# The head of a sorted-attention and gated-MLP kernel: another queue for one load, another order of the first keys, another spread of the first transposes

## The chip, the cores and the metric

The kernel runs on one core of a Trainium2 chip. The metric is the device time of one execution in microseconds. A core has TensorE (PE; its weight loads are listed as PEld), VectorE (DVE), ScalarE (ACT), GpSimd (POOL) and SyncE (SP), each with its own instruction stream in program order. Transfers are issued by SP, ACT and GpSimd and are carried out by 16 DMA engines.

## The reference

Four batches with eight heads each attend within eight blocks of 96 positions. An 8 by 8 matrix per head (`sort_net`) is balanced in five rounds and mixes the blocks of k and v; then every block of q attends to the mixed block of its own number. The result, as 3072 rows of 512, goes through an MLP with the gate h * cos(h).

```python
for _ in range(5):
    P = exp(P - max(P, -1)); P /= sum(P, -1) + 1e-9; P /= sum(P, -2) + 1e-9
k_sorted = einsum('bhij,bhjcd->bhicd', P, k_blocks)      # v the same
attn = softmax(q_blk @ k_sorted.T / sqrt(64))            # per block of 96
x = (attn @ v_sorted)  as [3072, 512]
h = x @ w_in                                             # [3072, 2048]
out = (h * cos(h)) @ w_out                               # [3072, 512]
```

## The kernel before

The 3072 rows are handled in eight groups `n` of 384 rows (one batch, four of its eight blocks). For every group the kernel makes the mixed keys and values it needs, transposes the query, computes scores (`qk`), the softmax (`expo`), the product with the values (`av`), a transpose of the result (`x_transpose`), and the two matrix products of the MLP (`up` and `down`). The order of instructions on every engine is written out by hand: the calls stand in the order in which the engines get their work. PSUM tiles come from two rotating pools, `big` (three tiles of two banks) and `acc` (two tiles of one bank); a new tile waits until the tile that had the buffer has been read.

The head, up to the first scores, is one chain:

- The sort matrices of batches 0 and 1 are loaded as two transfers of 64 rows, one issued on ACT and one on SP (L83), those of batches 2 and 3 as one of 128 rows, behind the first on ACT (L85). All go to `P_a`. VectorE then takes the maximum of each half `g` (L239, first g = 0, then g = 1), and only after that makes the masks from the identity.
- GpSimd issues the load of the first query rows (`load_q(0)`, L123), makes the identity (`make_identity`, in masks.py), issues the loads of k and v of batch 0 (`load`, L92), and clears the tail of three buffers (L195). All loads of GpSimd go through one queue, q0 in the profile.
- The balancing (L330 to L353) runs four passes, `it` = 0 to 3, for both halves: exponentials on ACT, column sums by a product on PE (`product`, L261), reciprocal and scaling on VectorE (`balance`). PE fills the gaps with transposes of the first query (`q_products`, L299; 32 in all, 16 for each half `z` of the heads), which ACT copies to `q_turned` during the last pass. The last pass ends with the spread weights of the first half (`spread(0)`, L280).
- The key blocks of group 0 are mixed on PE (`k_sort_0(t0, nt, engine, pool, tag)`, L361; `t0` and `nt` choose which of the 48 column tiles), and copied from PSUM to `kTs` with four copies per call by the engine named (the copies of ACT have line 286, those of VectorE line 288, whoever calls them). `v_turn` brings the weights for v into place (`bdv`, L437), `v_sort_b` mixes v (L451). `v_permute` on GpSimd (L176) rearranges half of v meanwhile. Then `qk(0, 0)` computes the first scores (L423).

Of the kernel before, what the change touches and what calls it, by code (L numbers as in the profile page):

```python
# [18 lines left out]
def kernel(  # L19
# [15 lines left out]
    nc = tc.nc  # L35
    B, H, S, D = q.shape
# [26 lines left out]
    big = ctx.enter_context(tc.tile_pool(name="big", bufs=3, space=bass.MemoryType.PSUM))  # L63
# [7 lines left out]
    vbuf, kbuf = kv[:, :CD], kv[:, CD:]  # L71
# [10 lines left out]
    for r, b in ((64, 0), (0, 1)):  # L82
        (nc.scalar, nc.sync)[b].dma_start(  # L83
            out=P_a[r:r + 64, 0], in_=sort_net[b].rearrange("h i j -> (h i) j"))
    nc.scalar.dma_start(  # L85
        out=P_a[:, 1], in_=sort_net[2:].rearrange("b h i j -> (b h i) j"))

    kin_d = k.rearrange("b h (j c) d -> b (h j) (c d)", j=nb)
    vin_d = v.rearrange("b h (j c) d -> b (h j) (c d)", j=nb)

    def load(buf, r, src):
        nc.gpsimd.dma_start(out=buf[r:r + 64], in_=src)  # L92
# [16 lines left out]
    def q_zeroed(n):  # L109

        return kbuf[:blk, :2 * (QZ + D)] if n % 2 else q_mem[:]
# [7 lines left out]
    def load_q(n):  # L119
        b, ih = n // 2, n % 2  # L120
        if n < NQ:

            nc.gpsimd.dma_start(  # L123
                out=q_rows, in_=q[b][:, ih * IC * blk:(ih + 1) * IC * blk].rearrange(
                    "h (p r) d -> p h (r d)", r=QR))
        else:
            src = q[b].rearrange("h (i c) d -> c i h d", c=blk).rearrange(
                "c i (h e) d -> c i h e d", e=2)
            q_heads = q_zeroed(n).rearrange("p (e x) -> p e x", e=2)[:, :, :QZ].rearrange(
                "p e (i h w) -> p i h e w", i=IC, h=H2)[:, :, :, :, :D]  # L130
            for i in range(IC):
                for e in range(2):
                    nc.gpsimd.dma_start(  # L133
                        out=q_heads[:, i, :, e], in_=src[:, ih * IC + i, :, e])

    def q_of(n, e):
        return q_turned[n % 2][:, e]
# [17 lines left out]
    def load_w_in(z):  # L155
        c = slice(z * Dff // 4, (z + 1) * Dff // 4)
        nc.gpsimd.dma_start(out=w_in_t[:, :, c], in_=w_in_d[:, :, c])

    def load_w_out(z):
        c = slice(z * FC // 4, (z + 1) * FC // 4)  # L160
        nc.gpsimd.dma_start(out=w_out_t[:, c], in_=w_out_d[:, c])
# [22 lines left out]
    kTs = const.tile([128, 3, 3, NB, HT], BF16, name="kTs")  # L184
    kT, kT2 = [kTs[:, :, 0], kTs[:, :, 2]], kTs[:, :, :2]

    load_q(0)
    make_identity(nc, ident[:])
    load(kbuf, 64, kin_d[0])
    load(vbuf, 0, vin_d[0])  # L190
    NP = 3
    p_bufs = []
    for i in range(NP):
        t = const.tile([blk, 2 * H2, 128], BF16, name=f"p_buf{i}")
        nc.gpsimd.memset(t[:, :, blk:], 0.0)  # L195
        p_bufs.append(t)
    vS[0] = const.tile([blk, 4 * NB, VW], BF16, name="vS")
    vS[1] = pair[:blk].rearrange("p (x w) -> p x w", w=VW)

# [59 lines left out]
    def product(lhs, rhs):  # L259
        ps = acc.tile([128, nb], FP32, name="sk", tag="acc")  # L260
        nc.tensor.matmul(  # L261
            ps[:], lhs.rearrange("p x j -> p (x j)"), rhs, start=True, stop=True)
        return ps
# [15 lines left out]
    def spread(g):  # L279
        nc.vector.scalar_tensor_tensor(  # L280
            bds[g][:], maskp.to_broadcast([128, 2 * H, nb]), ci[g][:], along(T[g]),
            op0=ALU.mult, op1=ALU.mult)

    def copy_on(eng, dst, src):
        if eng is nc.scalar:
            eng.copy(dst, src)  # L286
        else:
            eng.tensor_copy(dst, src)  # L288

    V, A = nc.vector, nc.scalar  # L290
# [3 lines left out]
    def q_products(n, z, lo, hi, pool, tag):  # L294
        if lo == 0:
            q_ps[n, z] = pool.tile([128, 2, IC, QR, blk // QR], BF16, name="qps", tag=tag)
        for i in range(lo, hi):
            e, hp, r = i // (2 * QR), i // QR % 2, i % QR
            nc.tensor.transpose(  # L299
                q_ps[n, z][hp * D:(hp + 1) * D, e, :, r],  # L300
                q_rows[:, (z * 2 + e) * 2 + hp, r * D:(r + 1) * D], ident[:blk, :blk])

    def q_turn(n, z, pool, tag, lo=0):
        q_products(n, z, lo, 4 * QR, pool, tag)
        ps = q_ps.pop((n, z))

        def place(hp, rows):
            dst = q_of(n, hp)[rows, :QW].rearrange("d (i h c) -> d h i c", h=H2, c=blk)
            return dst[:, z * 2:z * 2 + 2], ps[rows].rearrange("d e i r p -> d e i (r p)")

        if n == 0:
            return [place(0, slice(0, 128))]
        return [place(hp, slice(hp * D, (hp + 1) * D)) for hp in range(2)]
# [5 lines left out]
    def balance(g):  # L319

        nc.vector.scalar_tensor_tensor(
            T_eps[g][:], E_eps[g][:], 1.0, rr_one[g][:], op0=ALU.mult, op1=ALU.mult,
            accum_out=cs[g][:])
        nc.vector.reciprocal(ci[g][:], cs[g][:])
# [3 lines left out]
    for it in range(4):  # L328
        for g in range(NG):
            nc.scalar.activation(E[g], T[g], AF.Exp, scale=ci[g][:])  # L330
        nc.vector.tensor_copy(seen[:], E[0][:, :1])
        if it == 3:
            copy_on(A, *turned[0])
        sk = [product(same, E[g]) for g in range(NG)]
        if it == 1:
            q_products(0, 0, 0, 10, big, "big")
        elif it == 2:
            turned = q_turn(0, 0, big, "big", 10)
            q_products(0, 1, 0, 4, big, "big")
        elif it == 3:  # L340
            turned = q_turn(0, 1, big, "big", 4)
            copy_on(A, *turned[0])
        if it == 1:

            nc.gpsimd.tensor_copy(held[:], cs[1][:])
            for z in range(3):
                load_w_in(z)
            load_w_out(0)
        for g in range(NG):
            nc.vector.reciprocal(rr[g], sk[g][:])  # L350
            if it < 3 or g == 0:
                balance(g)
                if it == 3:  # L353
                    spread(0)
# [5 lines left out]
    def k_products(ps, t, c, rows, rhs, keys=kbuf):  # L360
        nc.tensor.matmul(  # L361
            ps[:, t], keys[rows, c * 2 * D:(c + 1) * 2 * D], rhs, start=True, stop=True)

    def k_sort_0(t0, nt, eng, pool, tag):

        ps = pool.tile([128, nt, 2 * MH], FP32, name="ks", tag=tag)
        for t in range(nt):
            k_products(ps, t, t0 + t, slice(64, 128),
                       bds[0][64:, H:, :IC])
        ms, ts = slice(0, MH), slice(t0, t0 + nt)  # L370
        psv = ps.rearrange("p t (e m) -> p e m t", e=2)
        for hp in range(2):
            for x in range(2):
                copy_on(eng, kT[0][hp * D:(hp + 1) * D, hp + x, ms, ts],
                        psv[x * D:(x + 1) * D, hp])
# [58 lines left out]
    def v_turn(eng=A):  # L434
        ps = big.tile([128, 128], FP32, name="bdp", tag="big")
        for r in (0, 64):
            nc.tensor.matmul(  # L437
                ps[r:r + 64], ident[:, 64 - r:128 - r], bds[0].rearrange("p x i -> p (x i)"),
                start=True, stop=True)
        copy_on(eng, bdv.rearrange("p x i -> p (x i)"), ps[:])  # L440
# [4 lines left out]
    def v_sort_b(b, d0, nd, eng, pool, tag):  # L445
        ps = pool.tile([128, nd, 2 * NB], FP32, name="vs", tag=tag)


        rows, xs = slice(0, 64 + b * 64), slice((1 - b) * H, (2 - b) * H)
        for t in range(nd):  # L450
            nc.tensor.matmul(  # L451
                ps[:, t], v_cols(d0 + t, b == 1 or d0 + t >= D // 2)[rows],
                bdv[rows, xs].rearrange("p x i -> p (x i)"), start=True, stop=True)
        copy_on(
            eng, vS[0][:, b * 2 * NB:(b + 1) * 2 * NB, d0:d0 + nd],
            ps[:blk].rearrange("p t n -> p n t"))
# [207 lines left out]
    B, C = (big, "big"), (acc, "acc")  # L664
# [27 lines left out]
        next(wz)  # L692

    k_sort_0(40, 8, V, *B)
    k_sort_0(0, 16, V, *C)
    v_turn()
    load_q(1)
    k_sort_0(32, 8, V, *B)
    load_w_in(3)
    k_sort_0(16, 16, A, *B)  # L700
    v_sort_b(0, 0, 8, A, *B)
    load_w_out(1)
    qk(0, 0)
# [241 lines left out]
```

## Time and profile before

| | us |
|---|---|
| median of 3 runs | 239.96 (239.51 to 241.65) |
| profiled execution, its own time | 241.18 |
| its span | 239.40 |
| PE busy in the span | 226.0 (94%) |
| VectorE busy | 175.8 (73%) |
| ACT busy | 155.3 (65%) |
| GpSimd busy | 87.7 (37%) |
| bytes read from and written to HBM | 27.27 and 6.29 MB |

All times of the trace count from the start of the span. A row of the timeline gives start, duration (of all instructions that were merged, if there are several), engine, line, operation, what is written and read, how many, and in brackets the idle time of the engine before it with what ended it. SPq, ACTq and POOLq rows are the issuing of transfers. A row of the chain of waits gives start, length, and the work that the end of the span waited for in that time.

### The profile page before, as it was taken

The page shows a single profiled execution, that of the slowest core. Times are in us where ns is not written, and L with a number is a line of the kernel's source. Part 1 is how long each engine was busy: PE and PEld are TensorE (multiplying, and loading weights), DVE is VectorE, ACT ScalarE, POOL GpSimd, SP SyncE. Part 2 cuts the span into 40 slices and gives each one's busy share as a digit, 9 for nine tenths or more (in the row PEclk, how much of TensorE's full clock was granted, in tenths as well). Part 3 has the DMA queues.
Part 4 walks back from the last instruction along what each step waited for, and adds up shares of the span by engine and source line. Part 5 has one row for each costly group of instructions (what it writes and reads, how often), then busy time and mean ns, then how long its engine had stood idle before and what let it go on. Part 6 is the DMA issues. An engine that isn't in the chain of part 4 may idle for free.

```text
span 239.4 us, 5344 instructions
## 1 busy us (share of the span) xinstructions
PE 226.0 (94%) x2148; PEld 148.1 (62%) x2169; DVE 175.8 (73%) x325; ACT 155.3 (65%) x217; POOL 87.7 (37%) x110
## 2 busy tenths in 40 slices
PE   2797999999999999999999999999999999999994
PEld 0777788956766566656566565655565566456554
DVE  3678977698879976895768986897789769635700
ACT  4355967785688946888578947683667376737611
POOL 6469953896960056990726200800000000000000
PEclk9999999999999999999999999999999999999999
DMA  6999999992999259786889769926671450251012
GB/s 82 213 198 205 207 210 219 212 158 89 132 152 162 66 138 191 122 179 154 117 115 126 79 136 140 189 43 99 136 212 33 102 181 0 49 140 44 0 47 89
DMA packets 66681, 30.90 MB, mean 129 GB/s; under 512 B 55392, under 2 KB 62176, under 8 KB 66400
## 3 DMA queue, kind: packets, MB, share of 16 engines
q0 software_dynamic: 24048, 13.64, 41.1%
q1 hardware_dynamic: 42096, 16.72, 29.8%
q8 instruction: 17, 0.28, 0.5%
q10 hardware_dynamic: 512, 0.20, 0.3%
q14 instruction: 8, 0.07, 0.1%
HBM read 27.27 MB, written 6.29 MB: 140 GB/s over the span
## 4 chain that ended last, share of the span: by engine, by line
PE 85%; DVE 7%; DMA 3%; ACT 2%; issue 1%; ACTq 0%; DVEq 0%
PE h L597 34%; PE o L629 31%; PE sc L428 4%; PE av L546 4%; PE ks L361 2%; DVE kTs L288 2%; PE xps L573 2%; PE pps L533 2%; PE vs L461 2%; DMA P_a<-in_sort_net_dram 2%; PE o L909 1%; PE sk L261 1%; PE qps L299 1%; DMA vperm<-p_buf 1%; PE vs L451 1%
## 5 line engine op out<-in xcount | busy, mean ns | idle before, releaser
L597 PE MATMUL h<-xT,w_in_t 128*128 128x384 bf16 (+1 forms) x576 | 91.2, 310 | 0.4 <-DVE xn L555 0.3
L629 PE MATMUL o<-w_out_t,gg 128*128 128x512 bf16 x347 | 85.1, 379 | 1.1
L604 ACT ACTIVATE c<-h,half_pi 128x768 f32<-128x768 f32 (+1 forms) x68 | 58.6, 864 | 26.8 <-PE h L597 25.6
L612 DVE TENSOR_TENSOR gg<-c,h 128x768 bf16<-128x768 f32 (+1 forms) x64 | 57.1, 899 | 22.2 <-ACT c L604 22.2
L597 PEld LDWEIGHTS <-w_in_t 128*128 128x128 bf16 x576 | 53.1, 98 | 27.1 <-issue 1.0
L629 PEld LDWEIGHTS <-gg 128*128 128x128 bf16 x368 | 33.1, 98 | 30.9
L489 DVE TENSOR_TENSOR s<-sc,mx 96x384 f32<-96x384 f32 (+1 forms) x43 | 32.2, 749 | 2.3
L483 DVE TENSOR_REDUCE mx<-sc 96x4 f32<-96x384 f32 (+1 forms) x43 | 31.9, 741 | 1.4 <-PE sc L428 0.7
L176 POOL COPY vperm<-kv 64x1536 bf16<-64x1536 bf16 (+1 forms) x10 | 28.0, 2843 | 1.1 <-DMA kv<-in_v_dram 1.1
L507 ACT ACTIVATE p_buf<-s 96x768 bf16<-96x768 f32 x32 | 26.0, 840 | 3.2 <-DVE s L489 2.9
L555 DVE TENSOR_TENSOR xn<-av,r 96x512 bf16<-96x512 f32 x32 | 22.0, 686 | 1.1
L133 POOL DMA_DIRECT2D kv<-in_q_dram x24 | 15.9, 671 | 0.8 <-issue 0.8
L428 PE MATMUL sc<-kTs,q_turned 128*128 128x96 bf16 x224 | 15.6, 206 | 0.0
L428 PEld LDWEIGHTS <-q_turned 128*128 128x128 bf16 x224 | 12.8, 98 | 4.0 <-DVE s L489 0.4
L553 DVE RECIPROCAL r<-av 96x8 f32<-96x8 f32 x32 | 6.4, 199 | 11.6 <-PE av L546 11.5
L286 ACT COPY kv<-o 128x512 f32<-128x512 f32 (+2 forms) x10 | 5.3, 531 | 14.3 <-PE o L629 12.7
L286 ACT CAST kTs<-ks 128x512 bf16<-128x512 f32 (+1 forms) x21 | 11.2, 539 | 3.7 <-PE ks L361 3.7
L133 POOL DMA_DIRECT2D q_mem<-in_q_dram x16 | 10.7, 684 | 2.6 <-DMA kv<-in_v_dram 2.3
L288 DVE COPY kv<-o 128x512 f32<-128x512 f32 (+1 forms) x5 | 3.0, 602 | 11.4 <-PE o L909 8.6
L286 ACT COPY xT<-xps 128x384 bf16<-128x384 bf16 (+1 forms) x10 | 5.1, 511 | 9.1 <-PE xps L573 9.1
L604 ACT ACT_TABLE_LOAD x8 | 10.3, 1283 | 0.1
L286 ACT COPY o_s<-o 128x512 f32<-128x512 f32 x9 | 5.3, 586 | 7.4 <-PE o L629 7.2
(105 smaller groups left out, 230.6 us busy)
## 6 DMA issues: line engine op xcount, KB each, us to landing
out_dram<-kv SPq DMA_DIRECT2D x12, 256.0 KB, 2.7
out_dram<-o_s SPq DMA_DIRECT2D x11, 256.0 KB, 2.4
w_in_t<-in_moe_w_in_dram POOLq DMA_DIRECT2D x4, 512.0 KB, 8.7
w_out_t<-in_moe_w_out_dram POOLq DMA_DIRECT2D x4, 512.0 KB, 12.6
kv<-in_k_dram POOLq DMA_DIRECT2D x2, 768.0 KB, 9.0
kv<-in_v_dram POOLq DMA_DIRECT2D x2, 768.0 KB, 12.5
pair<-in_k_dram POOLq DMA_DIRECT2D x2, 768.0 KB, 12.3
kv<-in_v_dram POOLq DMA_DIRECT2D x6, 256.0 KB, 6.3
```

The lines of the kernel that those rows point to most:

```text
L133: nc.gpsimd.dma_start(out=q_heads[:, i, :, e], in_=src[:, ih * IC + i, :, e])
L176: nc.gpsimd.tensor_copy(dst, src)
L286: eng.copy(dst, src)
L428: nc.tensor.matmul(out, q_of(n, hp)[:, x:x + 128], keys_of(n, u, h2, hp), start=True, stop=True)
L483: nc.vector.reduce_max(mx[:], scv, axis=AX.X)
L489: nc.vector.tensor_tensor(s, scv, mx.to_broadcast(list(s.shape)), op=ALU.subtract)
L507: nc.scalar.activation(p[:, :, :blk], s_t.pop((n, u)).rearrange("p e h c -> p (e h) c"), AF.Exp, scale=scale)
L555: nc.vector.tensor_tensor(xn.rearrange("p h e d -> p e h d"), avv[:, :, :, :D], r.to_broadcast([blk, 2, H2, D]), op=ALU.mult)
L597: nc.tensor.matmul(to, w_in_t[:, kk, f * 128:(f + 1) * 128], xT[n][:, kk, lo:hi], start=(kk == 0), stop=(kk == KC - 1))
L604: nc.scalar.activation(c[:, :, :x], h[:, :, :x], AF.Sin, bias=half_pi[:, 0:1])
L612: nc.vector.tensor_tensor(gate(n, fp)[:, :, lo:hi], c[:, :, :x], h[:, :, :x], op=ALU.mult)
L629: nc.tensor.matmul(o[:], gate(n, f // 2)[:, f % 2, ts * 128:(ts + 1) * 128], w_out_t[:, f, :], start=(f == 0), stop=(f == FC - 1))
```

## The change

Three things are changed.

- The third load of the sort matrix (L85) is issued by SP, behind SP's first, and not by ACT.
- `load_q(0)` and the loads of k and v are issued after the identity and after the clearing of the first of the three buffers; the other two are cleared after the loads. The loads keep their order.
- The transposes of the first query are spread as 4, 12, 10 and 6 over the passes 0 to 3, where it was 0, 10, 10 and 12. The order of the first keys is 40, 16, then the weights for v, then 0 and 32 (first column tile of each call), where it was 40, 0, weights, 32, 16. VectorE copies 40 and 0 and the weights for v, ACT copies 16 and 32; before, VectorE copied 40, 0 and 32, ACT the weights and 16. Calls 0 and 32 take their PSUM tiles from `acc`, 40 and 16 from `big`; before, only 0 was in `acc`. On GpSimd the order of instructions behind the first loads stays the same.

```diff
-    nc.scalar.dma_start(
+    nc.sync.dma_start(
         out=P_a[:, 1], in_=sort_net[2:].rearrange("b h i j -> (b h i) j"))
...
-    load_q(0)
     make_identity(nc, ident[:])
-    load(kbuf, 64, kin_d[0])
-    load(vbuf, 0, vin_d[0])
     NP = 3
     p_bufs = []
     for i in range(NP):
         t = const.tile([blk, 2 * H2, 128], BF16, name=f"p_buf{i}")
         nc.gpsimd.memset(t[:, :, blk:], 0.0)
         p_bufs.append(t)
+        if i == 0:
+            load_q(0)
+            load(kbuf, 64, kin_d[0])
+            load(vbuf, 0, vin_d[0])
...
-        if it == 1:
-            q_products(0, 0, 0, 10, big, "big")
+        if it == 0:
+            q_products(0, 0, 0, 4, big, "big")
+        elif it == 1:
+            turned = q_turn(0, 0, big, "big", 4)
         elif it == 2:
-            turned = q_turn(0, 0, big, "big", 10)
-            q_products(0, 1, 0, 4, big, "big")
+            q_products(0, 1, 0, 10, big, "big")
         elif it == 3:
-            turned = q_turn(0, 1, big, "big", 4)
+            turned = q_turn(0, 1, big, "big", 10)
             copy_on(A, *turned[0])
...
     k_sort_0(40, 8, V, *B)
+    k_sort_0(16, 16, A, *B)
+    load_q(1)
+    v_turn(V)
+    load_w_in(3)
     k_sort_0(0, 16, V, *C)
-    v_turn()
-    load_q(1)
-    k_sort_0(32, 8, V, *B)
-    load_w_in(3)
-    k_sort_0(16, 16, A, *B)
+    k_sort_0(32, 8, A, *C)
     v_sort_b(0, 0, 8, A, *B)
```

## The prediction

> **What bounds the kernel now.** I read the span by stages first, then the chain of waits, then the start in order of time.
>
> The view by stretches (time, then busy time of PE, PEld, DVE, ACT, POOL, granted clock, DMA share, GB/s) separates two regimes:
>
> ```profile
> 14.79:19.45 4.66, 2.92 (x60) 2.46 (x60) 4.00 (x12) 3.12 (x7) 4.66 (x3) 1.00 1.25 209
> 48.00:239.40 191.40, 186.82 (x1635) 113.79 (x1654) 141.10 (x215) 125.45 (x162) 54.95 (x64) 1.00 0.63 113
> ```
>
> From 48 us on, matrix work fills 186.82 of 191.40 us: nothing in the diff touches that part, so it can only be shifted. Between 14.79 and 19.45, where the first keys are made, VectorE is busy for 4.00 of 4.66 us and PE for 2.92. The chain of waits (start, length, what) says what holds this stretch and the one before it:
>
> ```profile
> 1.36 3.64 DMA P_a<-in_sort_net_dram
> 5.01 0.02 issue
> 5.03 0.16 DVE nmx L239
> ...
> 14.08 0.78 PE qps L299 x12
> ...
> 15.22 0.28 DVE kTs L288
> ...
> 19.45 0.49 PE sc L423 x7
> ```
>
> The chain begins with the third load of the sort matrix, passes twelve transposes of the query that stand ahead of the first keys, and then twelve VectorE copies of keys in a row. All three are on the path, so a microsecond taken there is one off the start of everything behind, unless something there is held by another clock (a transfer, GpSimd).
>
> **The third load.** It is issued at 1.36 on ACT, behind another; on SP it stands behind a load whose issue ends at 0.74 + 0.58 = 1.32, so it leaves no earlier than now. What changes is its company. DMA issues with microseconds to landing, then the packets, MB and share between 3 and 4 us (q0 carries GpSimd's loads, q10 ACT's):
>
> ```profile
> q_mem<-in_q_dram POOLq DMA_DIRECT2D x1, 384.0 KB, 5.6
> P_a<-in_sort_net_dram SPq DMA_DIRECT2D x1, 2.0 KB, 2.1
> P_a<-in_sort_net_dram ACTq DMA_DIRECT2D x1, 4.0 KB, 3.6
> ```
> ```profile
> q0 software_dynamic: 100, 0.05, 54.6%
> q10 hardware_dynamic: 26, 0.00, 3.5%
> ```
> ```profile
> 0.74 0.58 SPq L83 DMA_DIRECT2D P_a<-in_sort_net_dram  x1
> 0.82 0.06 DVE L206 MEMSET half_pi<- 128x1 f32 x1 [0.82 <-PEq L929]
> 1.30 0.90 POOL L123 DMA_DIRECT2D q_mem<-in_q_dram  x1 [0.85 <-POOLq L929]
> 1.36 0.86 ACTq L85 DMA_DIRECT2D P_a<-in_sort_net_dram  x1
> 2.50 0.29 POOL masks.py:199 TENSOR_SCALAR_AFFINE_SELECT ident<-ident 128x128 bf16<-128x128 bf16 x1
> 3.79 0.84 POOL L195 MEMSET p_buf<- 96x256 bf16 x3
> ```
>
> The small load on SP (L83) landed after 2.1 us, the third after 3.6, with its packets between the query's. In the changed kernel GpSimd first makes the identity (from the end of the query's issue, 1.30 + 0.90 = 2.20, to 2.50 + 0.29 = 2.79: 0.59) and clears one buffer (0.84 / 3 = 0.28), so the query's load leaves 0.87 later at most, at 2.17. GpSimd may start before 1.30, where it ends 0.85 us of idle time, since VectorE is let go at 0.82; then the query's load leaves as early as 0.82 + 0.59 + 0.28 = 1.69, 0.39 later. Either way the third load's packets have most of the engines to themselves. From both sides: with the small load's 2.1 plus the longer issue (0.86 - 0.58 = 0.28) it lands at 1.35 + 2.4 = 3.75; with nothing gained, at 1.35 + 3.64 = 4.99. I take 3.85, near the first end, because the rows to which it is then alike are the undisturbed ones: VectorE's first reduction moves from 5.03 to 3.87, **1.16 us**. ACT loses an issue of 0.86, which was covered by the same wait, so this counts nothing.
>
> [...]
>
> **The query's turns.** Per transpose: 0.78 / 12 = 0.065. Before, 10, 10 and 12 stood in passes two to four; now 4, 12, 10 and 6 in passes one to four.
>
> ```profile
> 9.33 1.18 PE L261 MATMUL sk<-E,same 128*128 128x8 f32 x4 [0.64 <-ACT E L330]
> 10.44 0.69 PE L299 MATMUL qps<-ident,q_mem 96*64 96x96 bf16 x10
> ```
> ```profile
> 14.15 0.35 DVE L280 SCALAR_TENSOR_TENSOR bd<-maskp,ci,T 128x128 bf16<-128x128 f32 x1
> 14.79 0.39 PE L361 MATMUL ks<-bd,kv 64*128 64x32 bf16 x8
> 14.89 0.80 ACT L286 COPY q_turned<-qps 128x768 bf16<-128x768 bf16 x1 [0.78 <-PE qps L299]
> 15.90 0.27 ACT L286 CAST bdv<-bdp 128x128 bf16<-128x128 f32 x1 [0.20 <-PE bdp L437]
> 16.84 1.50 ACT L286 CAST kTs<-ks 64x256 bf16<-64x256 f32 x4 [0.68 <-PE ks L361]
> ```
>
> The spread weights are ready at 14.50, yet the first key product starts at 14.79, behind the twelve. Six end at 14.08 + 0.39 = 14.47: product at 14.54, **0.25 gained**. The second pass gets two more than the ten that began at 10.44, 0.13 ahead of the third pass's products; the fourth pass has ten in front of it in either kernel, so much of this is waited for anyway, and I count 0.05 of the 0.13. The four of the first pass (0.26) fit into PE's idle 0.64 ahead of 9.33, if the query has landed: it lands at 1.69 to 2.17 plus 5.6 = 7.3 to 7.8, wanted at 9.33 - 1.16 - 0.26 = 7.9. That cover is thin; behind it stand the next products and with them both halves of the balancing. I put 0.1 for it.
>
> **The keys.** By shapes (mean ns last before the idle time):
>
> ```profile
> L288 DVE CAST kTs<-ks 64x128 bf16<-64x128 f32 x8 | 2.3, 289 | 0.7 <-PE ks L361 0.6
> L288 DVE CAST kTs<-ks 64x256 bf16<-64x256 f32 x4 | 1.7, 422 | 0.1
> ```
>
> On the clock of before, with the product at 14.54, the first copy starts 0.25 earlier, at 14.97. VectorE now has four short copies (4 x 0.30 with gaps = 1.20), the weights' copy for v (0.29, by the row of equal free size) and four long ones (4 x 0.43 = 1.72): ready at 18.18, scores at 18.22. ACT copies the query from 14.65 to 15.45, four long keys (1.50, to 16.95), then four short ones; between half of 0.375 and the whole they take 0.75 to 1.50, by the nearest row (0.27 for 128 elements) 1.1: ready at 18.05, at most 18.45. So both engines end together and scores move from 19.45 to about 18.25. Of this gain of 1.20, 0.25 is the one above; the order itself brings **0.95** (0.7 to 1.0). PE's v products wait for the weights' copy, now on VectorE, at 16.46; queued behind them are the scores, which at 18.25 leave them over 1.7 us.
>
> **What could be late next.** v and GpSimd's permutation of it:
>
> ```profile
> kv<-in_v_dram POOLq DMA_DIRECT2D x1, 768.0 KB, 11.0
> ```
> ```profile
> 14.77 5.45 POOL L176 COPY vperm<-kv 64x1536 bf16<-64x1536 bf16 x2
> 23.53 0.14 PEld L451 LDWEIGHTS <-vperm 64*128 64x128 bf16 x1
> 45.52 11.27 POOL L176 COPY vperm<-kv 64x1536 bf16<-64x1536 bf16 x4 [1.13 <-DMA kv<-in_v_dram]
> ```
>
> v landed at 14.3; behind a later query it lands at 14.7 to 15.2, so the permutation gains nothing and ends by 20.7, while its second half is wanted at about 23.53 - 2.2 = 21.3. The batch after that is ruled by the transfer's end (45.52), up to 0.9 later, and ends by 57.7; its reader:
>
> ```profile
> 62.07 0.40 PE L451 MATMUL vs<-bdv,vperm 128*128 128x64 bf16 x8
> ```
>
> At 59.9 after the shift it still has 2 us. So transfers do not take the gain back.
>
> **Sum.** 1.16 + 0.25 - 0.05 - 0.1 + 0.95 = 2.2 us off the profiled span, 239.40 to 237.2. The profiled execution itself took 241.18, the median of the runs shown is 239.96; the saving is in microseconds, so 239.96 - 2.2 = 237.8.
>
> **Rivals.**
> *The third load is no faster* (3.64 us is its own, not the query's doing). Then only 1.05 remains: 238.9. For it: its issue is longer than the small one's. Against it: the interleaved packets. 0.17.
>
> *PE's speed does not follow the work.* Two rows with the same eight products:
>
> ```profile
> 31.80 1.48 PE L597 MATMUL h<-xT,w_in_t 128*128 128x192 bf16 x8
> 34.08 0.83 PE L597 MATMUL h<-xT,w_in_t 128*128 128x192 bf16 x8
> ```
>
> PE is slow until about 33 us and 1.78 times as fast afterwards, though the granted clock is 1.00. If the switch stays where it is, 2.2 us of dense work come to lie in slow time and 2.2 - 2.2 / 1.78 = 0.97 is given back: 238.8, 0.12. If it comes as much earlier than the work, up to 0.97 more is won; with 0.8 of it, 237.0: 0.12. [...] The runs shown, 239.51 to 241.65, bear a spread of that size out.
>
> *Something later swallows it* (transfers, with a DMA share of 1.25 in the stretch above): 239.9, 0.06. Against it: the slack of 2 us above.
>
> *Slower: the query comes late and stalls the balancing.* PE works in order, so the four transposes of the first pass hold every later product. A later load of the same shape:
>
> ```profile
> DMA to landing us min/median/max: 10.5/10.5/10.5
> ```
>
> At 10.5 it would land at 2.17 + 10.5 = 12.7, 4.8 after 7.9: 239.96 - 2.2 + 4.8 = 242.6. It decides from a landing at 7.9 + 2.2 = 10.1, 7.9 us after the issue. Against it: that later load stood behind a full queue, and at the start there is none. 0.06.
>
> **Numbers.** The forecast as it stands: 0.47, own range 237.2 to 238.6. The range takes in the first rival with its bounds and most of the early switch: 236.6 to 239.4; outside are the swallowed gain, the stall and a little below. About 1% (2.4 us) is what a measurement can tell from no change, so faster means below 237.56: 0.2 from the forecast, 0.11 from the early switch, 0.02 from the rest, 0.33. Slower means above 242.36: 0.05 of the stall's cases. The rest, 0.62, is within 1%.
>
> **What would show it.** The first reduction of VectorE (L240 there) at about 3.9, not 5.0; no wait of PE ahead of the first transposes after about 7.9; the first key product within 0.1 us of the spread weights; key copies on both engines ending within 0.3 us of each other; the first scores near 17.2; the eight products of 192 columns turning fast near 31 us. It is wrong if the third load still takes 3.6 us, if PE waits for the query, or if the first scores come 2.2 us earlier and the end does not.

## The result and the profile after

| | before | after |
|---|---|---|
| median of 14 runs each, us | 239.96 (239.51 to 241.65) | 238.82 (238.29 to 239.30) |
| ratio | | 0.9935, 95% interval 0.9914 to 0.9956 |
| profiled execution, its own time | 241.18 | 239.25 |
| its span | 239.4 | 237.5 |

The kernel became faster by 0.65%, with an interval that leaves out 1: 1.14 us between the medians and 1.93 us between the profiled executions. The forecast was a saving of 2.2 us and a time of 237.8; the prediction gave 0.62 to a change of less than 1%, and this is one.

Both profiled spans are cut at the same six events: the reduction that waits for the third load, the first key product, the first scores (the row of the chain of waits; one score product runs ahead of it in both kernels), the first gate product, the next key products, the first output product. First the view by stretches of the kernel before (without 14.79 to 19.45, which the prediction shows), then that of the changed kernel (stretch, length, busy time of PE, PEld, DVE, ACT, POOL, granted clock, DMA share, GB/s):

```profile
0.00:5.03 5.03, 1.46 (x3) 0.28 (x3) 1.29 (x9) 1.77 (x4) 3.87 (x13) 1.00 0.41 46
5.03:14.79 9.76, 7.49 (x53) 6.61 (x53) 6.81 (x49) 3.73 (x12) 3.49 (x8) 1.00 1.09 212
19.45:31.80 12.35, 11.58 (x176) 10.55 (x176) 10.99 (x16) 9.27 (x15) 12.06 (x18) 1.00 1.30 214
31.80:38.33 6.53, 6.13 (x84) 5.38 (x82) 5.25 (x15) 4.19 (x7) 1.51 (x4) 1.00 1.07 193
38.33:48.24 9.91, 9.80 (x147) 9.16 (x148) 6.61 (x13) 7.96 (x12) 7.44 (x6) 1.00 1.08 218
48.24:239.40 191.16, 186.63 (x1634) 113.69 (x1653) 140.86 (x215) 125.21 (x162) 54.71 (x64) 1.00 0.63 113
```
```profile
0.00:3.56 3.56, 1.46 (x3) 0.28 (x3) 1.29 (x9) 1.59 (x3) 2.96 (x11) 1.00 0.11 9
3.56:13.22 9.66, 7.80 (x52) 6.79 (x53) 6.71 (x49) 4.01 (x15) 4.30 (x9) 1.00 1.08 201
13.22:16.86 3.64, 2.88 (x59) 2.42 (x60) 3.04 (x9) 3.39 (x10) 2.59 (x2) 1.00 1.14 189
16.86:29.30 12.44, 11.68 (x176) 10.59 (x177) 11.01 (x16) 9.69 (x16) 12.27 (x14) 1.00 1.27 205
29.30:36.35 7.05, 6.87 (x84) 6.06 (x82) 5.24 (x15) 4.20 (x7) 3.62 (x9) 1.00 1.14 214
36.35:46.26 9.91, 9.80 (x147) 9.16 (x147) 6.61 (x13) 7.95 (x12) 5.67 (x6) 1.00 1.11 215
46.26:237.50 191.24, 186.71 (x1634) 113.62 (x1653) 140.90 (x215) 125.12 (x162) 56.48 (x64) 1.00 0.64 115
```

Stretch by stretch, before to after: 5.03 to 3.56 (1.47 less, the third load), 9.76 to 9.66 (0.10 less, the query's turns), 4.66 to 3.64 (1.02 less, the order of the keys), 12.35 to 12.44, 6.53 to 7.05 (0.52 *more*), 9.91 in both, and 191.16 to 191.24. So the first scores come 2.59 us earlier, more than the 2.2 foreseen, and 0.69 of this is lost again, most of it in one stretch, 29.30 to 36.35, where the same work takes longer. The rest of the kernel is only shifted.

In the chain of waits (start, length, what) two of the three places of the change look as foreseen; the transposes of the query do so in part:

```profile
1.39 2.15 DMA P_a<-in_sort_net_dram
3.54 0.02 issue
3.56 0.16 DVE nmx L240
...
9.04 0.78 PE qps L300 x12
...
10.83 0.62 PE qps L300 x10
...
13.08 0.13 DVE rr L352
13.21 0.02 issue
13.22 0.80 PE ks L363 x24
...
16.38 0.44 DVE kTs L289
16.82 0.04 issue
16.86 0.57 PE sc L425 x6
```

The load still heads the chain, with 2.15 us and not 3.64, and four VectorE copies of keys lie in the last part, where twelve did. The transposes of the query no longer stand right ahead of the first key product, but they have not left the chain: twelve and then ten of them are on it in earlier passes. In the kernel before it was ten, in the row below, and then the twelve at 14.08.

```profile
12.31 0.62 PE qps L299 x10
```

The timeline of the changed kernel shows more of the prediction's signs:

```profile
1.53 0.91 POOL L123 DMA_DIRECT2D q_mem<-in_q_dram  x1
7.15 0.53 PE L300 MATMUL qps<-ident,q_mem 96*64 96x96 bf16 x4
12.73 0.35 DVE L281 SCALAR_TENSOR_TENSOR bd<-maskp,ci,T 128x128 bf16<-128x128 f32 x1
14.06 2.60 ACT L287 CAST kTs<-ks 64x256 bf16<-64x256 f32 x8
14.45 5.48 POOL L176 COPY vperm<-kv 64x1536 bf16<-64x1536 bf16 x2 [1.05 <-DMA kv<-in_v_dram]
15.07 1.74 DVE L289 CAST kTs<-ks 64x256 bf16<-64x256 f32 x4
```

The copies end at 14.06 + 2.60 = 16.66 on ACT and 15.07 + 1.74 = 16.81 on VectorE, 0.15 apart. The first transposes of the query at 7.15 have no wait in brackets: the query had landed (1.53 + 5.5 = 7.03). The spread weights are ready at 12.73 + 0.35 = 13.08, and the first key product follows at 13.22: 0.14 later, not within the 0.1 that was forecast. The permutation of v waits for v until 14.45 as it must.

What the profile does not show is that the profiled execution of before was no ordinary one. Beside the changed kernel and the experiments, the kernel before ran in four sets, 84 runs in all: 65 took 239.46 to 240.35 us (median 239.71), 19 took 241.05 to 241.79 (median 241.52), and none lay between. The first group is called ordinary here and the second late. The profiled one, 241.18, is of the late group. The changed kernel, in 14 runs here and 8 more below, never exceeded 239.51.

### The profile page after: what moved, and what is told of

It reads as the page before. It is cut to its first block, busy times and chain, and to the rows that moved or that the text cites. A ratio compares the mean times of both kernels' runs of the same rounds, so it can differ in the third digit from the quotient of the medians.

```text
span 237.5 us, 5344 instructions
## 1 busy us (share of the span) xinstructions
PE 227.2 (96%) x2148; PEld 148.9 (63%) x2169; DVE 174.8 (74%) x322; ACT 156.0 (66%) x220; POOL 87.9 (37%) x110
## 4 chain that ended last, share of the span: by engine, by line
PE 85%; DVE 5%; ACT 3%; DMA 3%; issue 1%; SPq 0%; ACTq 0%
PE h L599 35%; PE o L631 30%; PE sc L430 4%; PE av L548 4%; PE ks L363 3%; DMA vperm<-p_buf 2%; PE xps L575 2%; PE pps L535 2%; PE vs L463 2%; PE qps L300 2%; PE o L911 1%; PE sk L262 1%; PE vs L453 1%; DMA P_a<-in_sort_net_dram 1%; DVE s L491 1%
## 5 line engine op out<-in xcount | busy, mean ns | idle before, releaser
L631 PEld LDWEIGHTS <-gg 128*128 128x128 bf16 x368 | 33.1, 98 | 30.9
L287 ACT CAST kTs<-ks 128x512 bf16<-128x512 f32 (+2 forms) x25 | 12.2, 494 | 3.2 <-PE ks L363 3.0
```

The lines of the kernel that those rows point to most:

```text
L631: nc.tensor.matmul(o[:], gate(n, f // 2)[:, f % 2, ts * 128:(ts + 1) * 128], w_out_t[:, f, :], start=(f == 0), stop=(f == FC - 1))
```

## The experiments

Theory A: the third load, the order of the keys and the turns bring what the forecast gave them in every execution, and a part is lost to PE's speed switch. Rival B: the third load is late only in some executions, so the change of queue and of the query's load removes those, and the typical gain is the order of the keys alone. The first four kernels each make one part of the change to the kernel before; beside them it took 239.79 (25 runs, 239.48 to 240.34).

### Only the third load on SP

```diff
-    nc.scalar.dma_start(
+    nc.sync.dma_start(
         out=P_a[:, 1], in_=sort_net[2:].rearrange("b h i j -> (b h i) j"))
```

> Only the third load of the sort matrix is moved to SP; the query's load stays first on GpSimd. Theory (the query's packets delay the third load, the queue does not matter): the query is as early as before, so VectorE's reduction of the second half stays late, between 4.6 and 5.0 us, and the time is within 0.4 us of before. Rival (the load is delayed on ACT's queue itself): the reduction comes at 3.6 to 3.9 us, as in the changed kernel, the first scores about 1.3 us earlier than before (near 18.1), the time 1.0 to 1.5 us lower.

Measured: 240.09 (239.72 to 241.53, 10 runs), ratio 1.0024 [1.0004, 1.0045]: slower by a quarter of a percent, with an interval that just leaves out 1. Four of the ten took 241.16 to 241.53, the other six 239.72 to 240.12. Neither theory nor rival was met: in the trace, an ordinary run of 240.06 us, the reduction comes at 3.49, and the time is no lower. The new queue alone is no gain, and it brings the late executions to a chip on which the kernel before had none in 25 runs.

### Only the query's, k's and v's loads later

```diff
-    load_q(0)
     make_identity(nc, ident[:])
-    load(kbuf, 64, kin_d[0])
-    load(vbuf, 0, vin_d[0])
...
+        if i == 0:
+            load_q(0)
+            load(kbuf, 64, kin_d[0])
+            load(vbuf, 0, vin_d[0])
```

> Only the loads of the query, k and v are issued later on GpSimd (behind the identity and one cleared buffer); the third load stays on ACT. Theory (the query's packets delay the third load): the query is out of the way by 0.2 us only, since it left at 1.53 instead of 1.30 in the changed kernel, so the reduction comes earlier than 5.0 but how much is open: 3.6 to 4.4 us if the company alone decides, and the time 0.7 to 1.4 us lower. Rival (the queue decides): the reduction stays at 4.7 to 5.0 us and the time within 0.4 us of before. If both this run and the one with the load on SP stay late, the two edits are only worth something together.

Measured: 239.84 (239.30 to 240.07, 10 runs), ratio 0.9996 [0.9983, 1.0008]: the same, beside a kernel whose runs were all of the ordinary group. Both branches were written against the late profile and miss: in the trace the second reduction starts at 3.00 + 0.40 - 0.16 = 3.24, and there was nothing to win.

### Only the query's turns (4, 12, 10, 6)

```diff
-        if it == 1:
-            q_products(0, 0, 0, 10, big, "big")
+        if it == 0:
+            q_products(0, 0, 0, 4, big, "big")
+        elif it == 1:
+            turned = q_turn(0, 0, big, "big", 4)
         elif it == 2:
-            turned = q_turn(0, 0, big, "big", 10)
-            q_products(0, 1, 0, 4, big, "big")
+            q_products(0, 1, 0, 10, big, "big")
         elif it == 3:
-            turned = q_turn(0, 1, big, "big", 4)
+            turned = q_turn(0, 1, big, "big", 10)
```

> Only the transposes of the first query are spread anew (4, 12, 10, 6). Theory: the first key product follows the spread weights at once; from the reduction of the second half to the first key product it takes 9.5 to 9.7 us instead of 9.76, the first scores come 0.1 to 0.25 us earlier, the time is 0 to 0.25 us lower, which the measurement cannot tell from no change. Rival (the two transposes more in the second pass are paid in full, and four in the first): the same stretch takes 9.76 us or more and nothing is gained.

Measured: 239.52 (239.41 to 239.76, 10 runs), ratio 0.999 [0.998, 0.9999]: at most a few tenths. The theory's 9.5 to 9.7 us were not reached, from the second reduction to the first key product it is 9.81; but the rival's reason is not what the trace shows either. PE waits for the query:

```profile
7.36 0.53 PE L299 MATMUL qps<-ident,q_mem 96*64 96x96 bf16 x4 [0.32 <-DMA q_mem<-in_q_dram]
```

The trace shows something more: here the third load, on ACT as before and with the query's load as early as before, is not late (timeline and, second, DMA issues to landing).

```profile
1.30 0.90 POOL L123 DMA_DIRECT2D q_mem<-in_q_dram  x1 [0.85 <-POOLq L930]
1.34 0.60 ACTq L85 DMA_DIRECT2D P_a<-in_sort_net_dram  x1
3.19 0.24 DVE L239 TENSOR_REDUCE nmx<-P_a 128x1 f32<-128x8 f32 x2 [1.08 <-DMA P_a<-in_sort_net_dram]
```
```profile
P_a<-in_sort_net_dram ACTq DMA_DIRECT2D x1, 4.0 KB, 1.9
```

It lands after 1.9 us, not 3.6, and both reductions run in one go from 3.19. Nothing of this edit touches that load: it is how the ordinary group looks.

### Only the order and the engines of the keys

```diff
-    k_sort_0(0, 16, V, *C)
-    v_turn()
+    k_sort_0(16, 16, A, *B)
     load_q(1)
-    k_sort_0(32, 8, V, *B)
+    v_turn(V)
     load_w_in(3)
-    k_sort_0(16, 16, A, *B)
+    k_sort_0(0, 16, V, *C)
+    k_sort_0(32, 8, A, *C)
```

> Only the order of the first keys and the engines of their copies are changed. Theory: from the first key product to the second score product it takes 3.6 to 3.8 us instead of 4.66, so the scores start near 18.5 instead of 19.45, and 0.5 to 1.0 us of it is in the time. Rival (VectorE's and ACT's copies out of PSUM slow each other, or GpSimd's permutation, which starts no earlier, holds the later v products): the stretch is shorter but the first products of the gate do not come earlier than 31.4, and the time stays within 0.3 us.

Measured: 238.86 (238.61 to 238.99, 4 runs), ratio 0.9957 [0.994, 0.9973]. This one part reaches the time of the whole change. Its chain of waits from the first key product to the scores:

```profile
13.22 0.34 PE ks L361 x8
...
16.33 0.44 DVE kTs L288
16.77 0.04 issue
16.81 0.56 PE sc L423 x7
```

The first key product starts at 13.15 in its timeline, behind the last of the transposes; 3.66 us later come the scores, where the three kernels above with the old order take 4.65 to 4.67. Stretch and time (0.93 us lower between the medians) are as the theory had them.

### The late execution made on purpose

What makes a third load late? In the profile of before, ACT's issue of it took 0.86 us, in the ordinary execution above 0.60. The guess that was tried: of the two queues whose first loads start together at 0.75 one is served first, and the third load suffers when its queue is served second. So ACT's first load is held back by 0.17 us: it must wait for a VectorE instruction that clears the rows that it then writes.

```diff
+    nc.vector.memset(P_a[64:, 0], 0.0)
     for r, b in ((64, 0), (0, 1)):
```

> The kernel before, with one more store of zeros on VectorE that ACT's first load has to wait for, so that SP's first load is taken up ahead of ACT's; the rest is unchanged. Theory (the third load is late only in executions in which ACT's queue is served second, as in the profile of before: there SP's packets came first, the issue of the third took 0.86 us instead of 0.60 and it landed after 3.6 us instead of 1.9): the issue takes 0.8 to 0.9 us, the reduction of the second half comes at 4.6 to 5.3 us in the trace, and nearly all runs lie at 241.0 to 241.8 us. Rival (the late landing is chance, whatever the order): the reduction comes at 3.3 to 3.7 us and the runs lie at 239.5 to 240.5 with a few above 241.

Measured: 241.68 (241.12 to 242.52, 10 runs), ratio 1.0056 [1.0027, 1.0085] against a kernel before with 7 late executions among its 20 (median 240.01). All ten lie in the range of the late group or above it (three above 241.8). The issue took 0.74 us, a little less than expected; it also starts 0.15 later than in the profile of before, so the order and this delay come together here. The timeline:

```profile
1.29 0.90 POOL L124 DMA_DIRECT2D q_mem<-in_q_dram  x1 [0.83 <-POOLq L930]
1.51 0.74 ACTq L86 DMA_DIRECT2D P_a<-in_sort_net_dram  x1
5.05 0.16 DVE L240 TENSOR_REDUCE nmx<-P_a 128x1 f32<-128x8 f32 x1 [1.79 <-DMA P_a<-in_sort_net_dram]
```

The reduction at 5.05, and the scores at 19.47, are those of the profile of before (5.03 and 19.45). The packets by queue between 2.0 and 2.3 us (packets, MB, share; q1 is SP's queue, q10 ACT's), first in the ordinary execution with the new turns, then here:

```profile
q10 hardware_dynamic: 80, 0.00, 13.4%
```
```profile
q1 hardware_dynamic: 79, 0.00, 13.2%
```

In that window only ACT's first load moves in the one (80 packets) and only SP's in the other (79): in these two traces they are served one after the other, and the order differs. In the profile of before it is SP's too (74 packets, none of ACT's).

### The late execution with the query's load later

The same, and beside it the second edit (query, k and v issued later).

> The kernel before with both edits: SP's first load is forced ahead of ACT's by the store of zeros, and the loads of the query, k and v are issued later as in the changed kernel; the third load stays on ACT, turns and keys are the old ones. Theory (two things are needed for a late third load: its queue is served second, and the query's packets are already there): the third load lands after about 2.1 us, the reduction of the second half comes at 3.4 to 3.7 us instead of 5.05, and all runs lie at 239.5 to 240.6, against 241.1 to 242.5 with the forced order alone. Rival (the forced order alone makes it late): the reduction stays near 5 us and the runs above 241.

Measured: 240.00 (239.69 to 240.47, 10 runs, none late), ratio 0.9984 [0.9957, 1.0011]; the kernel before beside it had 8 late executions in 25 (median 239.74).

```profile
1.50 0.74 ACTq L86 DMA_DIRECT2D P_a<-in_sort_net_dram  x1
1.53 0.91 POOL L124 DMA_DIRECT2D q_mem<-in_q_dram  x1
3.47 0.16 DVE L241 TENSOR_REDUCE nmx<-P_a 128x1 f32<-128x8 f32 x1 [0.27 <-DMA P_a<-in_sort_net_dram]
```

The load leaves as late as in the kernel above (1.50 and 1.51, 0.74 each), and its reduction is at 3.47 instead of 5.05, as the theory had it. The two differ in the second edit alone. The ends of the two issues, trace by trace:

| trace | third load's issue ends | query's issue ends | reduction |
|---|---|---|---|
| before | 1.36 + 0.86 = 2.22 | 1.30 + 0.90 = 2.20 | 5.03 |
| ACT held back | 1.51 + 0.74 = 2.25 | 1.29 + 0.90 = 2.19 | 5.05 |
| only turns | 1.34 + 0.60 = 1.94 | 1.30 + 0.90 = 2.20 | with the first, from 3.19 |
| only the load on SP | 1.39 + 0.82 = 2.21 | 1.30 + 0.90 = 2.20 | 3.49 |
| ACT held back, query later | 1.50 + 0.74 = 2.24 | 1.53 + 0.91 = 2.44 | 3.47 |
| after | 1.39 + 0.82 = 2.21 | 1.53 + 0.91 = 2.44 | 3.56 |

In the two late traces, 1.5 to 1.8 us behind the others, the issue of the third load ends behind the query's, by 0.02 and 0.06 us. That does not decide by itself: in the kernel with only the load on SP it ends behind by 0.01, the trace is in time, and four of the ten runs were late. The packets tell more. Between 2.6 and 3 us (packets, MB, share), first in that kernel, then before:

```profile
q1 hardware_dynamic: 99, 0.00, 12.5%
```
```profile
q0 software_dynamic: 6, 0.00, 6.1%
```

In the first, 99 packets of the third load move in this window; in the second the query's begin (6) and none of the third load's move. Between 2.9 and 3.6 us it is 89 packets of the third load beside 60 of the query's in the first, 13 beside 76 before, and with ACT held back 3 beside 62. With ACT held back and the query later it is 126 beside 39. So in the two late traces few packets of the third load move beside the query's first ones, 3 and 13 against 89 and 126. What puts more of them there in one run and not in another, with issues that end this close together, is not shown.

### The change with the third load back on ACT, and the change again

```diff
-    nc.sync.dma_start(
+    nc.scalar.dma_start(
         out=P_a[:, 1], in_=sort_net[2:].rearrange("b h i j -> (b h i) j"))
```

> The changed kernel with the third load back on ACT's queue; the query's load stays later, turns and keys as changed. Theory (moving the load to SP costs 0.2 to 0.3 us, since SP's queue is the one served second in most executions): reduction at 3.2 to 3.3 us instead of 3.56, time 0.2 to 0.4 us below the changed kernel. Rival (the move is what makes the changed kernel's runs lie close together): the time is the same or higher and some runs lie above 240.

> The changed kernel once more, beside the others on this chip. Theory: 238.6 to 239.0 us, no run over 239.6, since its third load is never late. TensorE turns fast between 32 and 35.5 us, at another time than 33.07. Rival (the switch is tied to the work): it turns fast 3.6 to 3.9 us after the first gate product, as before.

Measured: 238.65 (238.40 to 239.31, 7 runs), ratio 0.9924 [0.989, 0.9957]; the change again 238.94 (238.43 to 239.51, 8 runs), 0.9916 [0.9887, 0.9945]. Once the query's load is later, the queue of the third load makes no difference that these runs separate. None of either is late. With the load back on ACT the reduction is at 3.45, not at the 3.2 to 3.3 of the theory: in that trace SP's first load is served first (76 packets of SP's queue and none of ACT's between 2.0 and 2.3 us), and ACT's issue of the third takes 0.86 us. So this load came second on either queue (on SP's behind 80 packets of ACT's in the changed kernel), and with the query later it was in time on both, 3.45 and 3.56.

The repeated profile of the same code tells more. Up to the first gate product it agrees with the first to 0.02 us (reduction 3.56, first key product 13.24 against 13.22, scores 16.87 against 16.86, gate product 29.29 in both), and yet the span ends at 236.9, not 237.5. The time is as expected; the moment at which PE turns fast is neither the theory's (32 to 35.5 us) nor the rival's (3.6 to 3.9 us behind the first gate product). PE's timeline, first of the profile after, then of the repetition:

```profile
29.29 1.48 PE L599 MATMUL h<-xT,w_in_t 128*128 128x192 bf16 x8
...
31.96 1.35 PE L599 MATMUL h<-xT,w_in_t 128*128 128x192 bf16 x8
...
33.40 0.83 PE L599 MATMUL h<-xT,w_in_t 128*128 128x192 bf16 x8
```
```profile
29.29 1.48 PE L599 MATMUL h<-xT,w_in_t 128*128 128x192 bf16 x8
...
31.66 0.83 PE L599 MATMUL h<-xT,w_in_t 128*128 128x192 bf16 x8
```

The second eight products take 1.35 us in one execution and 0.83 in the other: the switch to full speed came near 33.1 and near 31.2. (Sixteen transposes of the query take 0.86 us at 31.16 in the first and 0.56 at 31.17 in the second. The records of the granted clock in the first begin at 33.07; ahead of its first record a view shows 1.00.) The span is 0.6 us shorter for a switch 1.9 us earlier, about 0.3 us for each; this price rests on these two profiles.

### More warm-up work

`keep_warm(n)` issues idle PE products at the start. Eight instead of three in the changed kernel:

```diff
-    keep_warm(3)
+    keep_warm(8)
```

> The changed kernel with eight products on zeros at the start instead of three, which fill PE's idle time up to the first balancing product. [...]

Measured: 238.38 (238.25 to 238.55, 4 runs), ratio 0.9896 [0.9849, 0.9942]. Its view by stretches:

```profile
4.61:8.03 3.42, 2.26 (x16) 1.70 (x15) 2.51 (x21) 1.20 (x4) 0.68 (x3) 1.00 1.28 217
8.03:31.92 23.89, 22.14 (x307) 19.82 (x308) 19.18 (x57) 16.64 (x32) 19.89 (x25) 0.50 1.21 210
```

PE is granted full speed for 3.42 us early on, then half of it up to 31.92, though it is busy for 22.14 of those 23.89 us: slow again by the first scores, with a median 0.56 us below the changed kernel on the same chip. During the early stretch the balancing runs faster (the four products of its first pass take 0.75 us, 1.05 in the changed kernel), and the scores come at 16.44, not 16.87. The transposes find the query not yet there, 0.36 us for four where the changed kernel took 0.53 (timeline):

```profile
6.92 0.36 PE L300 MATMUL qps<-ident,q_mem 96*64 96x96 bf16 x4 [0.23 <-DMA q_mem<-in_q_dram]
```

Two more with eight warm-up products tried what this cover costs: the same with the third load on ACT, and that with the old turns of the query.

> The changed kernel with the third load back on ACT and eight products on zeros at the start. Theory: the gain of the eight products (0.4 to 0.6 us) stands, with the third load's reduction at 3.2 to 3.45 us: 238.1 to 238.5 us, the lowest so far or equal to the changed kernel with eight products. Rival (the four transposes of the first pass wait for the query, as with 0.23 us in that kernel, and take back what the earlier load gives): 238.4 to 238.8 us.

> The kernel before with the query's load later, the new order of the keys, and eight products on zeros at the start; the third load stays on ACT and the turns are the old 0, 10, 10 and 12. Theory (the new turns are worth 0.1 to 0.25 us, since the first keys follow the spread weights at once): 0.1 to 0.3 us above the kernel with the new turns beside it. Rival (without transposes in the first pass nothing waits for the query, and the new turns are worth nothing): equal or up to 0.2 us below.

Measured: 238.45 (238.13 to 239.20, 8 runs), 0.993 [0.990, 0.996], with PE waiting 0.44 us for the query; and 238.69 (238.21 to 239.28, 12 runs), 0.9935 [0.9911, 0.996]. The early stretch at full speed is in both traces, but, it seems, not in all runs: where a trace has it, the slow stretch behind it lowers the mean granted clock of the run to 0.95. This mean is 0.95 in all four runs of the kernel with the third load on SP, in four of eight with it on ACT, in six of twelve with the old turns, and 1.00 in the others. With the old turns the six took 238.21 to 238.69 and the other six 238.69 to 239.28, so the stretch goes with some 0.7 us there (medians 238.47 and 239.17); with the new turns, where the query is waited for, the two groups of four do not differ (medians 238.53 and 238.38). Theory and rival of the first are not told apart by 238.45; the 0.24 us of the second are in its theory's range, but the two groups mix in it. No version here is separated from the changed kernel by its interval (the last two ran on another chip than its repetition); the first has the lowest median.

## Why the prediction was right or wrong

**The time.** 238.82 lies in the range, 1.0 us above the forecast. It is above the forecast's own 237.2 to 238.6 and in the whole range because this takes in the first rival, whose reason is not the one found; so far that is luck. The step that failed is the last of the sum: "the saving is in microseconds, so 239.96 - 2.2 = 237.8". The saving was worked out against a profiled execution of 241.18 and taken off a median that did not have the stall in it. From the profiled execution it would have been 241.18 - 2.2 = 238.98, and its counterpart took 239.25. The three times given held the hint: 239.51, 239.96 and 241.65, with the profile at 241.18. The prediction took their spread for that of PE's switch; it was that of the two groups.

**The third load.** As a step for the profiled execution it was right in kind and too small: 1.47 us against 1.16; the load landed at 1.39 + 2.15 = 3.54, ahead of the better bound of 3.75. (The prediction calls the reduction that waits for it VectorE's first; it is the second, that of the other half was at 3.00.) "What changes is its company" is borne out by the two kernels with ACT held back, 5.05 and 3.47, that differ only in the second edit. What the step lacked is that the load is caught by this company in some executions only: by their times, in 19 of 84. In an ordinary execution the load has nothing to gain: the reduction was at 3.24 to 3.32 in the three traces that kept the load on ACT behind an undisturbed first one, and is at 3.56 in the changed kernel, about 0.25 later, where the load stands on the queue that came second and its issue takes 0.82 and not 0.60. So the second edit removes the late executions and the first does not; by itself the first is slower (1.0024). The first rival, a third load no faster, at 238.9, came within 0.1 us of the median, for another reason than it gave.

**The query's turns.** Net 0.1 was foreseen, and about 0.1 came. From the first product of the balancing to the first key product, the three traces with new turns and a later query take 8.51 to 8.53 us, those with the old turns 8.60 to 8.68. The parts are other than foreseen: the wait between the spread weights and the first key product fell from 14.79 - 14.50 = 0.29 to 0.14, so 0.15 was gained and not 0.25; and up to the spread weights it took 12.73 - 4.71 = 8.02 instead of 14.15 - 6.18 = 7.97, so 0.05 was paid in the passes and not 0.15. The stall that was the rival on the slower side did not come in the changed kernel, where the query landed at 7.03 and was wanted at 7.15. But it is near: the new turns alone wait 0.32 us for the query, which lands at 1.30 + 6.0 = 7.3 there, and so take 8.66; with PE faster the waits were 0.23 and 0.44. No run shows the 4.8 us that the rival gave the stall.

**The order of the keys.** 0.95 foreseen, 1.02 in the profile, and alone 0.99 to 1.01 us less than the kernels with the old order. ACT's eight copies took 2.60, as estimated (1.50 + 1.10). Of the typical gain this is nearly all: the ordinary group of before has a median of 239.71, and 239.71 - 1.0 + 0.25 - 0.1 = 238.86, an estimate from the keys, the later reduction and the turns.

**What comes late next.** Nothing: from the first output product to the end it is 191.16 and 191.24, and no transfer took the gain back.

**PE's speed.** The forecast let the switch follow the work, to near 31 us. In the profile after it came near 33.1, 0.4 us ahead of that of before (its records begin at 33.44) while the work came 2.5 us earlier, and 0.52 us was lost in that stretch; in the repetition it came near 31.2, and the same stretch, 29.29 to 35.82, took 6.53 us as in the kernel before, so nothing was lost in it. So the rival in which the switch does not follow is true of one execution and not of the next, and with 0.52 it cost half of its 0.97. Up to the first gate product the two profiles agree to 0.02 us, and their switches lie 1.9 us apart. In the profiles of before and after the records begin 33.44 - 31.80 = 1.64 and 33.07 - 29.29 = 3.78 us behind the first gate product. What sets the moment in one run was not tried.

**Open.** Why one of the two queues is served first, and why on some chips in a part of the runs and on one in none of 25, is not settled; the experiment fixed the order, with a delay of 0.15 us, and so shows the price of both, not the cause of the order. The link from a group of runs to the trace rests on one profile of each, and on the kernel in which all runs are late.

## What to carry to other kernels

A profile is one execution: put its own time beside all the run times before taking a saving from it, and if they fall into groups, find out which of them the profile shows and take the saving off that group alone. A stall on a small load can be there in a part of the executions only, here by their times in 19 of 84; what cured it here was to issue the large load later (the reduction at 3.47 and not 5.05 us), not to give the small one another queue (four of ten runs late). An edit that shares out copies between two engines so that both end together was predicted to 0.1 us from rows of the same shapes; a gain ahead of PE's switch to full speed should be given a spread of some 0.6 us, by which two profiles of one kernel differed here.

## What the runs showed of the hardware

Two loads of 2 KB issued on SP and ACT within 0.01 us were carried one after the other: between 2.0 and 2.3 us, 80 packets of ACT's queue and none of SP's moved with the new turns alone, with the load on SP alone, in the profile after and in its repetition; 74 and 76 of SP's and none of ACT's in the profile before and with the third load back on ACT. The next issue took 0.82 to 0.86 us in the five of these traces in which it stood on the queue that came second, and 0.60 in the one in which it stood on the other (the new turns alone).

A granted clock of 1.00 in a row does not mean that PE is at full speed: in the profile after the same eight products took 1.48 us at 29.29 and 0.83 at 33.40 under it, and the trace's own records begin at 33.07, between the two. With eight warm-up products the view shows 1.00 for 3.42 us (four transposes in 0.36 us), then 0.50 for 23.89 us with PE busy for 22.14 of them, and over the whole run a mean of 0.949.
